# Second expert's rows turned by DMA instead of on the matmul engine, and the second choice's first counts placed sooner

## The chip, the core and the metric

The kernel runs on one core of a Trainium2 chip. A core has a matmul engine (PE, with weight loads PEld beside it), a vector engine (DVE), an activation engine (ACT), GpSimd (POOL), a queue engine (SP) and 16 DMA engines, each with its own stream of instructions that runs in order; they wait for one another through semaphores. The metric is the device time of one execution in microseconds (us), as the median of several runs.

## What is computed

Attention over 8 batches, 12 heads, 448 positions and a head size of 64, then a layer of 8 experts over the 3584 resulting rows of 768 numbers. Each row goes to one expert, and each expert takes 448 rows; the order in which pairs of row and expert are granted is that of their gate logits, over all rows and experts at once.

```python
scores = cap * np.tanh(scale * np.matmul(q, k.transpose(0, 1, 3, 2)) / cap)
attn = np.exp(scores - np.max(scores, axis=-1, keepdims=True))
x = (attn / attn.sum(-1, keepdims=True)) @ v          # 3584 x 768 after reordering
logits = x @ w_gate                                    # 3584 x 8
for idx in np.argsort(-logits.flatten()):
    tok, e = idx // E, idx % E
    if assigned[tok] >= 0 or counts[e] >= N // E: continue
    assigned[tok] = e; counts[e] += 1
for e in range(E):
    mask = assigned == e
    out[mask] = np.maximum(x[mask] @ w1[e], 0) @ w2[e]  # w1: 768 x 1024, w2: 1024 x 768
```

## The kernel before

The first 330 us or so are attention, after which x lies in a DRAM tensor `xs` and the gate logits in SBUF. What follows is a loop over eight choices p = 0 to 7. A choice finds the expert that fills up next and its 448 rows; the expert's two layers are then computed. While PE does the matmuls of choice p, the other engines search for choice p+1 and fetch its weights and rows.

**The search** (class `Routing`) finds thresholds by counting: `select` runs three searches A, B and C. In each round, DVE (line 571) and ACT (line 565) compare all values with a few thresholds and count, one small matmul (line 577) sums the counts over partitions, and DVE (lines 581, 585) derives the next thresholds. Choices 0 and 1 use rounds with 3 thresholds, later ones with 7; `na` of the thresholds go to DVE, the rest to ACT. `finalise` then builds the list of rows: lines 692 and 716 on PE, last line 724, after which DVE writes `idx`.

**The rows of a choice** are gathered from `xs` by four indirect DMAs of POOL (`gather`, line 881) and must then be turned so that the 768 numbers lie on partitions. Two ways stand in the code. `xtr` (line 911) uses PE: four transposes into PSUM for each of six chunks, from which `cutx` (lines 939, 940) makes two float32r halves, `xgh` on ACT and `xgl` on DVE. The other way is used for choices from `FT` on (2 here): `planes` (line 919) lets ACT copy each of the four row tiles apart into 16-bit planes, sends them to DRAM tensors `xz`, and two transposing DMAs on SP (line 922) bring them back into `xg`; `cutt` (line 928 on ACT, then POOL for the first 256 rows and DVE for the rest) converts each of the two halves in two parts. The first matmul of an expert needs the first and the third of these four conversions.

**Each expert** has a first layer, `ffn1`: eight blocks of 18 matmuls of 448 columns (line 978; three products of high and low halves), and a second, `ffn2t`: six blocks of 24 (line 1040): 288 matmuls in all. The weight halves are split by `split1` and `split2` (ACT line 849, then POOL line 856).

**The order of all this is written by hand**, at build time. `tick` is called after each matmul and counts `now`, 320 counts to an expert (144 in the first layer, 176 in the second). The search is a Python generator; each `yield n` says after how many counts its next piece is to be put among the matmuls. `xq`, `bg`, `turnq` and `plan` hold the other pieces with their due counts. Since each engine runs its stream in order, a piece that stands too early in PE's stream makes PE wait. The search of choice 1 runs under expert 0, starting in `tx` and `first`, which turn the first expert's rows and begin its first block.

## Time and profile before

| what | us |
|---|---|
| median of 3 runs (835.54 to 835.95) | 835.9 |
| the profiled execution | 836.45 |
| its span, first to last instruction | 834.7 |
| PE busy in the span | 818.0 |
| DVE busy | 591.9 |
| ACT busy | 566.2 |
| POOL busy | 396.3 |

The profile tells when each instruction started and how long it was busy, and in brackets how long its engine had been idle before and which instruction ended that. The granted clock of PE stands beside each stretch. Matmuls overlap: one of 448 columns is busy for about 0.36 us, but its neighbours start 0.20 us after each other. So where PE is the limit, the distance between starts is what a matmul costs.

### The profile page before, as it was taken

What the parts mean: (1) busy time and instruction counts of PE and PEld (TensorE: products, weight loads), DVE (VectorE), ACT (ScalarE), POOL (GpSimd) and SP (SyncE); (2) the same over time, 40 slices, a digit from 0 to 9 for tenths busy, and PEclk for the clock granted to TensorE, in tenths of its full rate; (3) what the DMA queues carried; (4) which work ended last, traced back from release to release, by engine and by line L of the source; (5) the groups of instructions that cost most, each with busy time, mean ns of one, the idle gap of its engine ahead of it and who ended that gap; (6) DMA issues with size and microseconds to landing.
All of it is one profiled execution on the core that took longest, in us unless ns stands there. A gap on an engine that the chain in (4) does not pass through costs nothing.

```text
span 834.7 us, 16330 instructions
## 1 busy us (share of the span) xinstructions
PE 818.0 (98%) x5790; PEld 570.1 (68%) x5790; DVE 591.9 (71%) x1923; ACT 566.2 (68%) x749; POOL 396.3 (47%) x592
## 2 busy tenths in 40 slices
PE   7999999999999998999999999999999999999997
PEld 3333333333333336788888888888888899999997
DVE  2677899989989868868878779868868874353210
ACT  7999999999999954580783574754755845444510
POOL 8600000000000043591494696676686777787843
PEclk9999999999999999999999999999999999999999
DMA  6433354644635115815546978967968958959814
GB/s 245 159 107 133 111 155 130 203 120 147 200 111 155 41 28 151 293 60 186 167 149 237 256 208 259 321 225 201 300 203 246 294 179 255 317 194 253 254 67 132
DMA packets 116003, 155.55 MB, mean 186 GB/s; under 512 B 66834, under 2 KB 80370, under 8 KB 115922
## 3 DMA queue, kind: packets, MB, share of 16 engines
q1 hardware_dynamic: 108352, 125.19, 49.5%
q0 software_dynamic: 4832, 22.03, 7.9%
q10 hardware_dynamic: 2738, 7.31, 2.3%
q8 instruction: 45, 0.74, 0.4%
q14 instruction: 36, 0.29, 0.1%
HBM read 105.64 MB, written 40.60 MB: 175 GB/s over the span
## 4 chain that ended last, share of the span: by engine, by line
PE 90%; POOL 4%; DVE 3%; DMA 2%; issue 1%; ACT 1%; SPq 0%; DVEq 0%; POOLq 0%; ACTq 0%
PE psH L978 28%; PE psH L1040 24%; PE psX L201 13%; PE psS L161 13%; PE psM L235 3%; PE psS L156 1%; DMA xg<-xz 1%; PE psX L810 1%; POOL out_dram L998 1%; PE psM L257 1%; DVE cmpD L571 1%; PE psX L213 1%; POOL gw L95 1%; DVE cmpD L569 1%; DMA on<-yb 0%
## 5 line engine op out<-in xcount | busy, mean ns | idle before, releaser
L1040 PE MATMUL psH<-hh,w2h 128*128 128x448 f32 x720 | 199.1, 367 | 0.0
L162 ACT ACTIVATE e<-psS 128x896 f32<-128x896 f32 x168 | 146.0, 916 | 13.4 <-PE psS L161 8.7
L167 ACT ACTIVATE e<-e,bias 128x1792 f32<-128x1792 f32 (+2 forms) x74 | 147.2, 1990 | 0.8
L978 PE MATMUL psH<-xgh,w1h 128*128 128x448 f32 (+1 forms) x384 | 141.8, 369 | 0.9 <-ACT xgh L928 0.8
L1040 PEld LDWEIGHTS psH<-hh,w2h 128*128 128x128 f32 x720 | 134.1, 188 | 8.8 <-DVE hh L988 0.5
L978 PE MATMUL psH<-xgh,w1l 128*128 128x448 f32 (+1 forms) x384 | 139.9, 364 | 0.0
L856 POOL TENSOR_TENSOR w1l<-w1r,w1h 128x768 fp32r<-128x768 f32 x62 | 115.3, 1861 | 50.0 <-ACT w1h L849 45.0
L978 PE MATMUL psH<-xgl,w1h 128*128 128x448 f32 (+1 forms) x384 | 135.6, 366 | 0.0
L856 POOL TENSOR_TENSOR w2l<-w2r,w2h 128x768 fp32r<-128x768 f32 x64 | 132.6, 2073 | 6.0 <-ACT w2h L849 4.6
L161 PE MATMUL psS<-tq,tk 64*64 64x448 f32 x1200 | 130.4, 543 | 4.1 <-ACT e L162 4.1
L247 POOL COPY sm<-lgt 32x84 f32<-32x84 f32 x28 | 7.0, 249 | 251.3 <-DVE lgt L245 250.4
L1040 PE MATMUL psH<-hh,w2l 128*128 128x448 f32 x360 | 124.3, 367 | 0.0
L201 PE MATMUL psX<-e,nv 64*64 64x448 f32 x1176 | 121.8, 536 | 0.0
L161 PEld LDWEIGHTS psS<-tq,tk 64*64 64x64 f32 x1200 | 41.4, 132 | 74.6 <-issue 44.3
L201 PEld LDWEIGHTS psX<-e,nv 64*64 64x64 f32 x1176 | 45.7, 133 | 64.8 <-issue 62.5
L978 PEld LDWEIGHTS psH<-xgh,w1h 128*128 128x128 f32 x384 | 72.4, 189 | 6.6 <-ACT xgh L928 1.9
L849 ACT ACTIVATE w2h<-w2r 128x768 fp32r<-128x768 f32 x64 | 76.6, 1210 | 0.3
L978 PEld LDWEIGHTS psH<-xgh,w1l 128*128 128x128 f32 x384 | 72.3, 188 | 4.5
L978 PEld LDWEIGHTS psH<-xgl,w1h 128*128 128x128 f32 x384 | 72.2, 188 | 4.4 <-DVE xgl L940 0.2
L1040 PEld LDWEIGHTS psH<-hh,w2l 128*128 128x128 f32 x360 | 67.6, 188 | 4.2
L987 ACT ACTIVATE hh<-psH 128x448 fp32r<-128x448 f32 x56 | 30.2, 539 | 58.4 <-PE psH L978 55.6
L1044 DVE STREAM_TRANSPOSE yq<-psH 128x448 f32<-128x448 f32 x45 | 35.5, 789 | 37.1 <-PE psH L1040 36.6
(407 smaller groups left out, 1295.3 us busy)
## 6 DMA issues: line engine op xcount, KB each, us to landing
w1r<-in_moe_w_dram SPq DMA_DIRECT2D x64, 384.0 KB, 4.7
w2r<-in_moe_w_dram SPq DMA_DIRECT2D x64, 384.0 KB, 5.5
nv<-in_v_dram SPq DMA_DIRECT2D x24, 448.0 KB, 5.6
tk<-in_k_dram SPq DMA_DIRECT2D x23, 448.0 KB, 3.4
tq<-in_q_dram SPq DMA_DIRECT2D x23, 448.0 KB, 4.3
yb<-yq SPq DMA_DIRECT2D x60, 168.0 KB, 4.5
xs<-Y SPq DMA_DIRECT2D x28, 336.0 KB, 4.5
on<-yb SPq DMA_DIRECT2D x7, 1152.0 KB, 7.5
```

The source lines that it names most:

```text
L95: nc.gpsimd.tensor_copy(gw[hp,p,c:c+8],wgs[hp,p,:])
L161: nc.tensor.matmul(ps[w:w+64,h,:S],tks[g,0][hp,o,r*64:r*64+64],tks[g,1][hp,o,:],start=True,stop=True)
L162: nc.scalar.activation(ev(g,r),ps[:,:,:S],AF.Tanh,scale=sr[0])
L167: act=lambda: nc.scalar.activation(e,e,AF.Exp,scale=sr[1],bias=bias)
L201: for h in range(2): nc.tensor.matmul(avp[g,o][h*64:h*64+64,:S],z[w,r,h,:],ev(g,r)[w,h,:],start=r==0,stop=r==6)
L235: nc.tensor.matmul(ps[k*32:k*32+32,c],lhs,rhs[:,c],start=x<4 and i==0 and b<B-1,stop=b<B-1 and c.stop==S and x==max(y for y in range(end) ...
L849: nc.scalar.activation(view(h),r,AF.Copy)
L856: (eng or nc.gpsimd).tensor_tensor(view(l),r,view(h).bitcast(F32),op=ALU.subtract)
L978: nc.tensor.matmul(ps[:,o:C],a[:,c,:],b[:,c,o:],start=(m==0 and o==0),stop=(m==DC*3-1)); m+=1
L987: nc.scalar.activation(h,ps[:,:C],AF.Relu)
L1040: nc.tensor.matmul(ps[:,:C],spl[p,2,hf,f//2][w][:,f%2,cc*128:cc*128+128],h[a][:,f],start=(m==0),stop=(m==nm-1))
L1044: turnq.append((now[0]+5,now[0]+(5 if p==E-1 else TL),lambda: nc.vector.transpose(yq[p][:,:,hf,cc::3],ps[:,:C])))
```

## The change

`FT` becomes 1: choice 1 also takes the DMA way, and the six calls of `xtr(1, ...)` go. Several places that named choices relative to `FT` now name them directly, so that later ones keep theirs; what follows `FT` still is that choice 1 loads three first-layer weights as soon as its expert is known (`early`), that its first block takes the products without `xgl` first, that choice 2 loads two and not three so early, and that choice 2 now does all counts of its first three A rounds on DVE with longer gaps, as later choices did.

The search of choice 1 does all three counts of each first round (A, B, C) on DVE, places the summing matmul sooner, and loses one count of distance in later rounds. Its keys (`propose_b`) are made, and its first counts started, while the first expert's rows are still being turned; the split of the first expert's second weight tile moves from DVE to POOL.

```diff
-LK=(0,0,112,112,112,112,112,112); FT=2
+LK=(0,0,112,112,112,112,112,112); FT=1
...
-            m=R[i]-1; alone=s.cur>FT and ab=="A" and i<3; na=m if alone else 5 if m==7 else s.na
+            m=R[i]-1; alone=s.cur>FT and ab=="A" and i<3; na=m if alone or s.cur==1 and not i else 5 if m==7 else s.na
...
-            s.pos='A'; yield max(6,12-s.since()) if s.cur==1 and s.since()<20 else 16 if m==7 and s.place()>304 else (24 if s.place()<8 else 18) if m==7 and s.cur==FT+1 and s.place()<32 else 16 if m==7 and s.cur==FT and s.place()<32 else max(13,18-s.since()) if m==7 and s.since()<20 else s.hA+1*(s.cur==1)+(3 if m==7 else 0)+((9 if s.cur>FT+2 and i==1 else 5) if alone and i else 0); s.pos=''
+            s.pos='A'; yield 5 if s.cur==1 and not i else max(6,12-s.since()) if s.cur==1 and s.since()<20 else 16 if m==7 and s.place()>304 else (24 if s.place()<8 else 18) if m==7 and s.cur in (2,3) and s.place()<32 else max(13,18-s.since()) if m==7 and s.since()<20 else s.hA+(3 if m==7 else 0)+((9 if s.cur>4 and i==1 else 5) if alone and i else 0); s.pos=''
...
-                split1(p,1,nc.vector)
+                split1(p,1)
+                rt.propose_b(0,rt.NC)
                 first(n)
         for c in range(n): cutx(p,c,ps[c],256,C)
+        step()
...
                 xtr(0,c+4)
-                if c==1: rt.propose_b(0,rt.NC)
...
-            if p==1 and f==0: work[1]=[lambda: xtr(1,4)]; work[4]=[lambda: xtr(1,5)]
...
-            plan+=[(126,lambda: split1(1,0)),(144,lambda: split1(1,1))]
-            plan+=[(x,lambda c=c: xtr(1,c)) for x,c in ((156,0),(164,1),(172,2),(175,3))]
+            pass
```

On PE, at the end of expert 0's second layer (line 1040, now 1041) and the start of expert 1's first (line 978, now 980), the order before was this; `xg_3569` and `xg_3570` are the two gathered halves of expert 1's rows:

```order
L911 MATMUL psX<-ident,xg_3569 128x128 x2
L911 MATMUL psX<-ident,xg_3570 128x128 x2
L1040 MATMUL psH<-hh,w2l 128x448
L577 LDWEIGHTS r_bo
L577 MATMUL psR<-r_cd_358,r_bo 128x4
L978 MATMUL psH<-xgh,w1h 128x448
L911 MATMUL psX<-ident,xg_3569 128x128 x2
L911 MATMUL psX<-ident,xg_3570 128x128 x2
L978 MATMUL psH<-xgl,w1h 128x448
L978 MATMUL psH<-xgh,w1l 128x448
```

and now, at the same place on PE:

```order
L1041 MATMUL psH<-hh,w2l 128x448
L1041 MATMUL psH<-hh,w2h 128x448 x2
L1041 MATMUL psH<-hh,w2l 128x448
L980 MATMUL psH<-xgh,w1h 128x448
L980 MATMUL psH<-xgh,w1l 128x448
```

The transposes are gone, and the first block begins with the products that need only `xgh`.

On ACT, from the last count of choice 1's search to the end of expert 0's second layer, the order before was this (line 565 are counts, 849 weight splits, 939 conversions of turned rows):

```order
L565 ACTIVATE cmpA,r_cd_357<-r_qt,r_HC 128x252
L565 ACTIVATE cmpA,r_cd_358<-r_VAt,r_T8A 128x252
L849 ACTIVATE w1h<-w1r 128x768
L565 ACTIVATE cmpA,r_ce_350<-r_VAt,r_H8A 128x252 x2
L849 ACTIVATE w1h<-w1r 128x768
L565 ACTIVATE cmpA,r_ce_351<-r_VAt,r_H8A 128x252 x2
L939 ACTIVATE xgh<-psX 128x448 x2
L565 ACTIVATE cmpA,r_cd_358<-r_VAt,r_H8A 128x252
L939 ACTIVATE xgh<-psX 128x448 x3
```

and now, on ACT from the same count on:

```order
L565 ACTIVATE cmpA,r_cd_357<-r_qt,r_HC 128x252
L921 ACTIVATE xgh<-xg_3569 128x1536
L922 DMA xz_61<-xgh 128x1536
L921 ACTIVATE xgl<-xg_3569 128x1536
L922 DMA xz_61<-xgl 128x1536
L921 ACTIVATE xgh<-xg_3570 128x1536
L922 DMA xz_62<-xgh 128x1536
L921 ACTIVATE xgl<-xg_3570 64x1536
L849 ACTIVATE w1h<-w1r 128x768 x2
L565 ACTIVATE cmpA,r_cd_358<-r_VAt,r_H8A 128x252
L930 ACTIVATE xgh<-xg_3569 128x3x256 x2
L930 ACTIVATE xgh<-xg_3570 128x3x192 x2
```

The plane copies (line 919, now 921) and the four conversions (928, now 930) have come in, the conversions in a row; the counts of choice 2's first A rounds have gone from ACT.

On DVE, at the start of expert 0, the order before was this (line 940 subtracts for `xgl`, lines 519 to 531 are `propose_b`, 571 counts):

```order
L856 TENSOR_TENSOR w1l<-w1r,w1h 128x768
L940 TENSOR_TENSOR xgl<-psX,xgh 128x192 x2
L940 TENSOR_TENSOR xgl<-psH,xgh 128x192 x2
L940 TENSOR_TENSOR xgl<-psX,xgh 128x448 x2
L519 TENSOR_SCALAR r_Bt<-r_b 112x32
L520 TENSOR_SCALAR r_Ct<-r_c 112x32
L521 TENSOR_TENSOR r_VB<-r_P,r_Bt 112x256
L522 TENSOR_TENSOR r_VC<-r_P,r_Ct 112x256
L523 TENSOR_TENSOR r_K_372<-r_At,r_Bt 112x32
L531 SCALAR_TENSOR_TENSOR r_K_373<-r_kk,r_Ct 112x32
L571 TENSOR_SCALAR cmpD,r_cd_357<-r_VAt,r_T0A 128x224 x2
```

and now, on DVE at the same place:

```order
L519 TENSOR_SCALAR r_Bt<-r_b 112x32
L520 TENSOR_SCALAR r_Ct<-r_c 112x32
L521 TENSOR_TENSOR r_VB<-r_P,r_Bt 112x256
L522 TENSOR_TENSOR r_VC<-r_P,r_Ct 112x256
L523 TENSOR_TENSOR r_K_372<-r_At,r_Bt 112x32
L531 SCALAR_TENSOR_TENSOR r_K_373<-r_kk,r_Ct 112x32
L942 TENSOR_TENSOR xgl<-psX,xgh 128x192 x2
L942 TENSOR_TENSOR xgl<-psH,xgh 128x192 x2
L571 TENSOR_SCALAR cmpD,r_cd_357<-r_VAt,r_T0A 128x224 x3
L942 TENSOR_TENSOR xgl<-psX,xgh 128x448 x2
```

The counts stand ahead of the last two subtractions, and there are three of them instead of two.

## Rows read from the trace of the kernel before

**Rows 1.** The page's first part: busy time, share, instructions of each engine.

```profile
PE 818.0 (98%) x5790; PEld 570.1 (68%) x5790; DVE 591.9 (71%) x1923; ACT 566.2 (68%) x749; POOL 396.3 (47%) x592
```

**Rows 2.** Timeline of PE, end of expert 0: start us, us busy, instruction, count.

```profile
402.32 0.60 PE L911 MATMUL psX<-ident,xg 128*128 128x128 f32 x4
402.68 0.45 PE L1040 MATMUL psH<-hh,w2l 128*128 128x448 f32 x1
402.96 0.57 PE L1040 MATMUL psH<-hh,w2h 128*128 128x448 f32 x2
```

**Rows 3.** Timeline of PE, expert 1's first matmul and its eighth.

```profile
407.49 0.45 PE L978 MATMUL psH<-xgh,w1h 128*128 128x448 f32 x1
...
409.81 0.37 PE L978 MATMUL psH<-xgh,w1h 128*128 128x448 f32 x1
```

**Rows 4.** Timeline of POOL, first gather of expert 1's rows; in brackets idle before.

```profile
389.24 0.98 POOL L881 DMA_INDIRECT xg<-xs,idx  x1 [13.73 <-DVE zz L734]
```

**Rows 5.** Timeline of POOL, ACT and PE: expert 2's rows (choice 2).

```profile
446.70 0.98 POOL L881 DMA_INDIRECT xg<-xs,idx  x1 [3.70 <-DVE zz L734]
...
466.53 0.84 ACT L928 ACTIVATE xgh<-xg 128x768 fp32r<-128x768 f32 x1 [2.12 <-DMA xg<-xz]
...
468.40 1.98 ACT L928 ACTIVATE xgh<-xg 128x768 fp32r<-128x768 f32 x3
...
468.89 0.37 PE L1040 MATMUL psH<-hh,w2l 128*128 128x448 f32 x1
469.85 0.47 PE L978 MATMUL psH<-xgh,w1h 128*128 128x448 f32 x1 [0.60 <-ACT xgh L928]
```

**Rows 6.** Timeline of POOL, SP and ACT: the rows of choice 6, the seventh.

```profile
684.50 0.99 POOL L881 DMA_INDIRECT xg<-xs,idx  x1 [2.81 <-DVE zz L734]
...
696.76 6.33 SPq L922 DMA_TRANSPOSE xg<-xz  x2
...
702.93 1.58 ACT L928 ACTIVATE xgh<-xg 128x768 fp32r<-128x768 f32 x2 [5.40 <-DMA xg<-xz]
705.17 1.26 ACT L928 ACTIVATE xgh<-xg 128x576 fp32r<-128x576 f32 x2 [0.66 <-DMA xg<-xz]
```

**Rows 7.** Timeline of POOL and ACT: the rows of choice 7, the eighth.

```profile
742.53 0.98 POOL L881 DMA_INDIRECT xg<-xs,idx  x1 [2.27 <-DVE idx L728]
...
764.41 1.26 ACT L928 ACTIVATE xgh<-xg 128x576 fp32r<-128x576 f32 x2 [0.76 <-DMA xg<-xz]
```

**Rows 8.** Timeline of POOL, ACT, PE: choice 3 (the fourth); then the fifth's first matmul.

```profile
506.05 0.98 POOL L881 DMA_INDIRECT xg<-xs,idx  x1 [2.48 <-DVE zz L734]
...
523.91 0.85 ACT L928 ACTIVATE xgh<-xg 128x768 fp32r<-128x768 f32 x1 [0.17 <-DMA xg<-xz]
...
530.68 0.47 PE L978 MATMUL psH<-xgh,w1h 128*128 128x448 f32 x1
...
592.33 0.47 PE L978 MATMUL psH<-xgh,w1h 128*128 128x448 f32 x1 [0.22 <-ACT xgh L928]
```

**Rows 9.** Timeline of DVE and PE, start of expert 0: subtractions, a count, summing matmul.

```profile
345.53 1.38 DVE L940 TENSOR_TENSOR xgl<-psX,xgh 128x448 fp32r<-128x448 f32 x2 [0.72 <-ACT xgh L939]
...
347.91 0.44 DVE L571 TENSOR_SCALAR_CACHE_REDUCE cmpD<-r_VAt,r_T0A 128x224 bf16<-128x224 f16 x1
...
348.27 0.37 PE L978 MATMUL psH<-xgh,w1l 128*128 128x448 f32 x1
348.78 0.18 PE L577 MATMUL psR<-r_cd,r_bo 128*128 128x4 bf16 x1
```

**Rows 10.** Attention matmuls early and late; windows: length, busy by engine, then PEclk.

```profile
4.81 2.47 PE L156 MATMUL psS<-tq,tk 64*64 64x448 f32 x16
...
284.48 1.68 PE L156 MATMUL psS<-tq,tk 64*64 64x448 f32 x16
...
829.30:832.30 3.00, 0.00 (x0) 0.00 (x0) 0.00 (x0) 0.49 (x1) 2.03 (x3) 1.00 0.39 146
832.40:834.70 2.30, 0.00 (x0) 0.00 (x0) 0.00 (x0) 0.00 (x0) 0.00 (x0) 0.50 0.15 53
```

More of the change, by code (lines that the diff above doesn't have):

```diff
@@ L948, in tick @@
         if bc[0]>=BG:
-            if pend and not (cur[0]==FT-1 and 166<now[0]%320<316): bc[0]=0; scatter(*pend.pop(0))
+            if pend and not (cur[0]==1 and 166<now[0]%320<316): bc[0]=0; scatter(*pend.pop(0))
         if len(res)>cur[0]+1 and cur[0]+1 not in xgs:
@@ L955, in tick @@
                 o=(n-1)*320; g=now[0]-o; a=max(262,g+92); b=max(284,g+118)
-                bg.extend((o+x,o+min(y,316),z) for x,y,z in ((a,a+18,lambda: cutt(n,0,0,3)),(a,a+34,lambda: cutt(n,0,3,6)),(b,b+(0 if n==FT else 26),lambda: cutt(n,1,0,3)),(b,b+(7 if n==FT else 22),lambda: cutt(n,1,3,6))))
+                bg.extend((o+x,o+min(y,316),z) for x,y,z in ((a,a+18,lambda: cutt(n,0,0,3)),(a,a+34,lambda: cutt(n,0,3,6)),(b,b+(0 if n<3 else 26),lambda: cutt(n,1,0,3)),(b,b+(7 if n<3 else 22),lambda: cutt(n,1,3,6))))
         while xq and xq[0][0]<=now[0]: xq.pop(0)[1]()
```

## The prediction

> **What bounds the kernel now.** I read the page's busy shares first: the matmul engine (PE) is busy for 98% of the span [rows 1], so time can come from work taken off PE, or from the few waits it still has. Next I read PE's timeline where one expert hands over to the next. At the handover to the second expert there is no wait worth the name: the matmuls of expert 1's last blocks run on, with groups of four transposes (line 911) between them [rows 2, 3]. At the handover to the third, where the rows already come turned by DMA, PE sits idle for 0.60 us until ScalarE (ACT) has converted them [rows 5]. That is the path the second expert is about to get: index found, gather on GpSimd (POOL), four plane copies on ACT, DMA out, transposing DMA back, conversion on ACT, first matmul. The question of this case is how long that path is, against the PE work left when it starts.
>
> **What the change takes off PE.** Six calls of four transposes go, 24 in all. One call stands on PE from 402.32 to the next matmul's start at 402.68, which is 0.36, and the matmul behind it hands on after 0.28 (402.68 to 402.96) where the usual step is 0.20 [rows 2]. So a call costs 0.44 us. Four of the six lie before the second expert's first matmul (407.49): 1.76 us. The other two lie behind it: from 407.49 to 409.81 seven matmuls start, which take 1.40 us by themselves, so the two calls and a short wait cost 0.92 [rows 3]. Together 2.7 us leave PE. The ACT and DVE work of the six conversions was beside PE work and is worth nothing here.
>
> **When the new path starts.** In the order of PE's instructions the last routing matmul of the second choice (L724) stands after 206 matmuls of the first expert before, and after 197 now: nine matmuls of 0.20, or 1.8 us. The gather then starts at 389.24 - 1.8 = 387.4 [rows 4]. I take the whole 1.8: the routing steps stand nine matmuls apart or more in the first layer now as before, and seven or eight apart at the start of the second in both, so each count has the time that it had.
>
> **How long the new path is.** No row shows it for the second choice; the same path of later choices does. From the first gather to the first matmul that it allows: third choice 446.70 to 469.85, 23.15 us, with two counts of the next search standing on ACT between the first conversion and the other three, where the rows leave 1.0 us (466.53 + 0.84 to 468.40) [rows 5]. Seventh choice: 684.50 to the end of the third of four conversions, 705.17 + 1.26/2 = 705.8, which is 21.3 [rows 6]. Eighth: 742.53 to 764.41 + 0.63, which is 22.5 [rows 7]. Fourth: its first conversion started 17.9 us after its gather (506.05 to 523.91) [rows 8]; with the 2.9 us that the seventh needs from first to third conversion (702.93 to 705.8), 20.7. The second choice is most like the seventh and the eighth: in the new order its four conversions stand in a row on ACT, with no count between. I take their middle, 21.9, and keep 20.7 and 23.15 as ends.
>
> **The wait that results.** PE would reach the second expert's first layer at 407.49 - 1.76 = 405.7, 18.3 us after the gather. The path ends at 387.4 + 21.9 = 409.3. So PE waits for 3.6 us (2.4 to 4.9). Before, with its two late calls counted in, that layer stood as if begun at 407.49 + 0.92 = 408.4. **The handover costs +0.9 us** (-0.3 to +2.2): the 2.7 us that were saved are waited away, and some more. Behind the waiting instruction stand the second expert's matmuls and the routing steps between them; ACT waits on the same DMA with nothing else that PE needs, SP holds its next weight loads behind the transposing DMAs as it does for every later choice, and the expert's first two weight splits stand ahead of the conversions on ACT and POOL.
>
> **Later handovers.** The third choice's L724 moves from 177 matmuls to 180 (0.6 us later), the fourth's from 167 to 177 (2.0), the fifth's from 152 to 162, the sixth's from 146 to 150; the rest stay. Third: from the gather to the point where PE would have gone on (468.89 + 0.20 = 469.09) there were 22.4 us, now 21.8, against a path of 20.7 + 1.0 (the two counts between) to 23.15: a wait of 0 to 1.35, in the middle 0.7, where it was 0.76 [rows 5]. That is -0.1 (-0.8 to +0.6). Fourth: its first matmul came at 530.68 with no idle shown, 22.6 us after a gather at 506.05 + 2.0 [rows 8]; its conversions now stand on ACT as the third's did, so the same path gives 0 to 0.5; I take +0.2. The fifth's handover had 0.22 idle on ACT [rows 8], which may go or double; fifth and sixth start their gathers after 162 and 150 matmuls, with 25 us and more left: 0 +/- 0.2.
>
> **The start of the first expert.** The second choice's first count moves ahead of matmul work, and a routing matmul that came 0.51 after its neighbour, not 0.20 (348.27 to 348.78), should come freely: -0.3 at best. Against it three counts of 0.44 at most now stand on DVE ahead of two subtractions that PE needs; DVE had 0.72 idle there, so these come at most 0.6 late [rows 9]. The second weight split goes from DVE to POOL, ahead of the third that POOL did before, and isn't needed until the second block. I take -0.1 (-0.3 to +0.6).
>
> **Sum:** +0.9 - 0.1 + 0.2 + 0 - 0.1 = +0.9 us. The profiled execution took 836.45 us (span 834.7 and 1.75 around it), so 837.35 by it; it lay 0.55 above the median of the three runs, 835.9. The forecast for the median is 836.8.
>
> **Rivals.** *The clock falls in the wait (slower).* This trace shows PE's granted clock at 1.00 until 832.30 and at 0.50, the lower level of 1.2 GHz, from 832.40 on, after PE had been without a matmul since 829.30 [rows 10]. The wait forecast here, 2.4 to 4.9 us, is longer than any that the rows above show inside the expert part. If the clock falls in that wait, the expert's first matmuls take 0.40 instead of 0.20. For how long is bounded by nothing at one end, and at the other by the start of the kernel: sixteen attention matmuls took 2.47 us at 4.81 where they take 1.68 later [rows 10] and that stands in the kernel's first 7.3 us; as much time at the lower level again would cost up to 3.6 us. I take 2.4, the cost of the first two thirds of that: 839.2 us. It decides from a wait near the long end. The Trainium skill states the same direction (TensorE: Matmul & The Clock Gate, Part 1, "The HAM clock gate"): the throttled clock is the default and only activity holds it off. By that rule alone the wait would cost the clock as well; the rows leave it open for a wait of this length, so it is a rival and not the forecast.
>
> *The path is as long as the third choice's* at every handover (23.15): +2.2, +0.6 and +0.5, less 0.1 at the start: +3.2, 839.1. It speaks for it that three weight loads go out shortly before the gather, as there; against it, that no writes of finished rows run beside it.
>
> *The rows come in time (faster)*: then the transposes' 2.7 us is all gain, 833.2. It needs a path of 18.3, which none of the four rows comes near. The Trainium skill (DMA: Bandwidth & Descriptors, "Latency and other measured facts") gives a transposing DMA 261 GB/s; the two here carry 786 KB and 590 KB, so I estimate 5.3 us by that page, and the sum would be about 3 us lower. The trace doesn't agree: from their start at 696.76 to the third conversion at 705.17 it took 8.4 us [rows 6].
>
> *The change doesn't do what it says*: the earlier counts aren't ready when PE reaches them and PE waits there, so the gather starts no sooner; +1.8, 838.6. Against it: the spacing is one that held before.
>
> **How the numbers follow.** Forecast 0.58; clock 0.20; long path 0.10; rows in time 0.07; no sooner start 0.05. A measurement of this kernel tells about 0.2%, 1.7 us, from no change. The forecast's own bounds reach from about 835.3 to 838.2; nearly all of it lies within 0.2%. Faster 0.08 (the rows in time, and a bit), same 0.56, slower 0.36 (clock, long path, half of the rest). The range leaves out the rows in time at the lower end, and at the upper a fallen clock on top of a long path: 835.3 to 839.6.
>
> **What would show it.** In the new profile: no line 911 transposes at 402 to 410; the second choice's gather near 387.4; the first conversion 17.5 to 20 us behind it; an idle row of 2.4 to 4.9 us before the second expert's first matmul, put down to ACT; steps of 0.20 right behind it if the clock held, 0.40 if not; the third expert's wait at 0 to 1.4 us. I am wrong if that idle is under 2 us, or if PE waits before line 577 in the first expert.

## The result and the profile after

The changed kernel takes 841.4 us (median of 5 runs, 839.8 to 842.5) against 835.9 (835.5 to 836.6) before: ratio 1.006, 95% interval 1.0049 to 1.0072. It is slower by 5.5 us, where 0.9 was forecast, and lies beyond the range. The profiled execution took 841.39 us, its span is 839.6; before 836.45 and 834.7, so the traces differ by 4.95. Of all executions behind this document one, of 2098.5 us in the run that takes the causes away with the early DMA, lies far from the others and is left out of its median.

The start of the first matmul of each layer, read from both timelines of PE, gives the length of every layer, with the wait that ends it:

| stage, us | before | after | difference |
|---|---|---|---|
| up to the first expert's first layer | 343.67 | 344.01 | +0.34 |
| first expert, first layer | 30.95 | 31.90 | +0.95 |
| first expert, second layer | 32.87 | 34.47 | +1.60 |
| second expert, first layer | 31.02 | 31.74 | +0.72 |
| second expert, second layer | 31.34 | 31.04 | -0.30 |
| third expert, both | 60.83 | 60.59 | -0.24 |
| fourth expert, first layer | 30.31 | 33.09 | +2.78 |
| fourth expert, second layer | 31.34 | 30.31 | -1.03 |
| all behind | 242.34 | 242.47 | +0.13 |

The first row is no effect of the change that PE shows: up to there it waits nowhere anew, and the kept traces of all versions spread from 342.50 to 344.21 at this point. PE's row of the page says that PE does less and the span is longer, so what came is waiting (before it was [rows 1]):

```profile
PE 817.2 (97%) x5766; PEld 568.7 (68%) x5766; DVE 594.8 (71%) x1934; ACT 567.4 (68%) x735; POOL 402.4 (48%) x598
```

**The second expert's handover** is where I looked first, in PE's timeline (start, us busy, instruction; in brackets the idle time before and its releaser):

```profile
406.62 0.37 PE L1041 MATMUL psH<-hh,w2l 128*128 128x448 f32 x1
410.38 0.74 PE L980 MATMUL psH<-xgh,w1h 128*128 128x448 f32 x1 [3.38 <-ACT xgh L930]
410.92 0.57 PE L980 MATMUL psH<-xgh,w1l 128*128 128x448 f32 x1
411.29 0.57 PE L980 MATMUL psH<-xgh,w1h 128*128 128x448 f32 x1
...
413.16 0.41 PE L980 MATMUL psH<-xgh,w1l 128*128 128x448 f32 x1
413.41 0.18 PE L577 MATMUL psR<-r_cd,r_bo 128*128 128x4 bf16 x1
413.45 0.45 PE L980 MATMUL psH<-xgh,w1h 128*128 128x448 f32 x1
```

PE waits 3.38 us for the conversion. Behind the wait the steps are 0.37 (410.92 to 411.29), not the usual 0.20. The windows of this stretch (length, busy of PE, PEld, DVE, ACT, POOL, then granted clock) say why: the clock went to its lower level, 1.2 GHz, within the wait, and came back at 413.3.

```profile
407.00:409.80 2.80, 0.00 (x0) 0.00 (x0) 0.00 (x0) 1.74 (x3) 1.35 (x1) 1.00 1.14 231
409.90:413.20 3.30, 2.82 (x8) 2.48 (x8) 2.84 (x2) 2.90 (x4) 3.30 (x5) 0.50 0.95 331
413.30:416.00 2.70, 2.65 (x14) 2.09 (x13) 2.65 (x5) 0.00 (x0) 2.70 (x3) 1.00 1.01 396
```

**DVE stands still while POOL subtracts.** At the start of the first expert, DVE, POOL and PE:

```profile
342.72 0.43 DVE L521 TENSOR_TENSOR r_VB<-r_P,r_Bt 112x256 f16<-112x256 f16 x1
343.06 2.03 DVE L522 TENSOR_TENSOR r_VC<-r_P,r_Ct 112x256 f16<-112x256 f16 x1
...
342.79 2.03 POOL L856 TENSOR_TENSOR w1l<-w1r,w1h 128x768 fp32r<-128x768 f32 x1 [0.24 <-ACT w1h L849]
...
345.63 0.36 PE L980 MATMUL psH<-xgl,w1h 128*128 128x192 f32 x1 [0.93 <-DVE xgl L942]
```

Line 522 does the same work as line 521 in the row above and takes 2.03 us instead of 0.43. It ends 0.27 after POOL's subtraction. The subtraction for which PE waits 0.93 us stands behind it. At the second expert the two DVE subtractions of line 932 (0.75 each where nothing is beside them) take 4.65 us, all of it beside POOL:

```profile
410.36 4.65 DVE L932 TENSOR_TENSOR xgl<-xg,xgh 128x576 fp32r<-128x576 f32 x2 [4.63 <-ACT xgh L930]
...
410.25 1.83 POOL L937 TENSOR_TENSOR xgl<-xg,xgh 128x768 fp32r<-128x768 f32 x1
412.02 0.09 POOL L854 MEMSET gap<- 1x1 f32 x1
412.07 2.32 POOL L856 TENSOR_TENSOR w1l<-w1r,w1h 128x768 fp32r<-128x768 f32 x1
```

At the fourth expert the same pair takes 4.20 us, and PE waits 0.94 us for it, then 0.88 and 0.41 for counts queued behind it on DVE. Before, the pair took 1.43 there (first line below), because the rows came earlier and POOL was done.

```profile
530.71 1.43 DVE L930 TENSOR_TENSOR xgl<-xg,xgh 128x576 fp32r<-128x576 f32 x2 [0.18 <-issue]
...
533.65 4.20 DVE L932 TENSOR_TENSOR xgl<-xg,xgh 128x576 fp32r<-128x576 f32 x2 [0.65 <-issue]
...
533.07 1.85 POOL L937 TENSOR_TENSOR xgl<-xg,xgh 128x768 fp32r<-128x768 f32 x1 [0.64 <-ACT xgh L930]
534.86 0.09 POOL L854 MEMSET gap<- 1x1 f32 x1
534.95 2.29 POOL L856 TENSOR_TENSOR w1l<-w1r,w1h 128x768 fp32r<-128x768 f32 x1
...
538.00 0.85 PE L980 MATMUL psH<-xgl,w1h 128*128 128x448 f32 x3 [0.94 <-DVE xgl L932]
```

Not every DVE instruction is held. The counts of line 571, with one input, keep their 0.44 us beside POOL:

```profile
525.82 0.44 DVE L571 TENSOR_SCALAR_CACHE_REDUCE cmpD<-r_VAt,r_H8A 128x224 bf16<-128x224 f16 x1
...
525.40 1.85 POOL L856 TENSOR_TENSOR w1l<-w1r,w1h 128x768 fp32r<-128x768 f32 x1
```

The Trainium skill has this rule (SBUF — State Buffer, "Who interferes with whom"): DVE and POOL share a pair of ports, a DVE instruction with two SBUF inputs contends with a POOL instruction that reads SBUF, and "the other fully blocks" for the whole instruction. The rows above agree: line 522 took 2.03 us instead of 0.43, and line 571, with one input, kept its 0.44. I had not weighed it.

### The profile page after: what moved, and what is told of

Read it like the earlier page. It is cut to its first block, busy times and chain, and to the rows that moved or that the text cites. A ratio compares the mean times of both kernels' runs of the same rounds, so it can differ in the third digit from the quotient of the medians.

```text
span 839.6 us, 16298 instructions
## 1 busy us (share of the span) xinstructions
PE 817.2 (97%) x5766; PEld 568.7 (68%) x5766; DVE 594.8 (71%) x1934; ACT 567.4 (68%) x735; POOL 402.4 (48%) x598
## 4 chain that ended last, share of the span: by engine, by line
PE 89%; POOL 4%; DVE 3%; DMA 1%; issue 1%; ACT 1%; SPq 0%; POOLq 0%; ACTq 0%; DVEq 0%
PE psH L980 28%; PE psH L1041 25%; PE psX L201 13%; PE psS L161 13%; PE psM L235 3%; PE psS L156 1%; PE psX L810 1%; POOL out_dram L999 1%; PE psM L257 1%; DMA xg<-xz 1%; PE psX L213 1%; POOL gw L95 1%; DVE cmpD L569 0%; DMA on<-yb 0%; PE psR L577 0%
## 5 line engine op out<-in xcount | busy, mean ns | idle before, releaser
L856 POOL TENSOR_TENSOR w1l<-w1r,w1h 128x768 fp32r<-128x768 f32 x63 | 117.9, 1872 | 40.8 <-ACT w1h L849 35.2
L988 ACT ACTIVATE hh<-psH 128x448 fp32r<-128x448 f32 x56 | 30.1, 537 | 52.7 <-PE psH L980 49.5
```

What stands on the lines that cost most here:

```text
L856: (eng or nc.gpsimd).tensor_tensor(view(l),r,view(h).bitcast(F32),op=ALU.subtract)
L988: nc.scalar.activation(h,ps[:,:C],AF.Relu)
```

## Experiments

Theory 1: the loss has four parts: the wait, the low clock in it, DVE held by POOL at three places, and the fourth expert's later rows. Rivals: the clock alone, the search order, or a lateness that has nothing to do with POOL. Each median is of 4 to 11 runs; the kernel before lay at 835.5 to 836.5 beside them, and the ratio is to it, with its 95% interval. Each trace is of one execution.

### The start: split back on DVE; small operations later

```diff
-                split1(p,1)
+                split1(p,1,nc.vector)
```

> The changed kernel with one thing undone: the second split of the first expert's weights is on VectorE again, as before, and GpSimd has nothing in that stretch. Theory 1 (VectorE's write of VC, 2.03 us where it took 0.42 before, was held for as long as GpSimd's subtraction of 2.03 us ran beside it): VC takes 0.4 to 0.5 us again; VectorE does the split itself (0.95), so the two subtractions of 128x192 end 0.5 to 0.7 us sooner, TensorE's wait of 0.93 shrinks to 0.2 to 0.5, and the time falls by 0.4 to 0.8 us, to about 840.8. Rival (the sooner order of the choice's work on VectorE is the cost, GpSimd is not): VC stays at 2 us or the wait stays at 0.9 or grows by the 0.95 that VectorE now does more, and the time is 841.4 to 842.4.

Median 839.6 (ratio 1.0051, 1.0037 to 1.0064). Line 522 is back at 0.42 and the wait at 0.40:

```profile
343.54 0.42 DVE L522 TENSOR_TENSOR r_VC<-r_P,r_Ct 112x256 f16<-112x256 f16 x1
...
344.48 0.36 PE L980 MATMUL psH<-xgl,w1h 128*128 128x192 f32 x1 [0.40 <-DVE xgl L942]
```

The first layer took 31.39 us, 0.5 less, as expected. It isn't the 30.95 of before: the wait of 0.40 is left, and it stands in every run that has the small operations ahead of the subtractions and the split on DVE. The median fell by 1.8; of that, 0.9 is in the first expert's second layer (33.59, rows sooner in that execution) and 0.6 lies ahead of the first expert, so neither is an effect of the split that is shown.

```diff
-                rt.propose_b(0,rt.NC)
                 first(n)
         for c in range(n): cutx(p,c,ps[c],256,C)
+        rt.propose_b(0,rt.NC)
         step()
```

> The changed kernel with the six small operations of the second choice (Bt to K) on VectorE behind the subtractions of 128x192 and no longer ahead of them; GpSimd's split stays. Theory 1: VC may still be held by GpSimd's subtraction, but nothing that TensorE waits for stands behind it; the wait of 0.93 at the first expert's fifth matmul goes and the time falls by 0.6 to 1.0 us, to about 840.5. Rival (something else holds the subtraction, its planes or TensorE's transposes): the wait stays above 0.7 and the time is the changed kernel's within 0.3 us.

Median 842.4 (1.0089, 1.0075 to 1.0103): worse, so my expectation failed. Line 522, now later, met POOL's next split and was held again. The first count stood behind it, PE waited 1.71 us for that, and the clock fell (DVE, POOL, PE, then a window):

```profile
344.72 2.06 DVE L522 TENSOR_TENSOR r_VC<-r_P,r_Ct 112x256 f16<-112x256 f16 x1
...
344.55 1.95 POOL L856 TENSOR_TENSOR w1l<-w1r,w1h 128x768 fp32r<-128x768 f32 x1 [0.78 <-ACT w1h L849]
...
348.14 0.16 PE L577 MATMUL psR<-r_cd,r_bo 128*128 128x4 bf16 x1 [1.71 <-DVE cmpD L571]
349.20:352.50 3.30, 3.30 (x9) 2.95 (x10) 1.61 (x9) 2.52 (x5) 0.68 (x1) 0.50 1.01 397
```

The hold stands, the cure was none: what counts is which instruction is behind the held one.

### POOL's splits held away; matmuls in the wait; both

```diff
-                xq.extend(((n-1)*320+248+8*f,lambda f=f: split1(n,f)) for f in range(2))
+                xq.extend(((n-1)*320+248+8*f,lambda f=f: split1(n,f)) for f in range(3 if n==1 else 2))
...
+            if (p,f)==(3,1): work[1]=[lambda: split1(3,2)]
+            if p in (1,3) and f<2: at={**at,0:[],1:[(4,0)]+at[1]}
```

> The changed kernel with GpSimd's splits of weights (w1l of the third chunk, w2l of the first) taken from beside the subtractions on VectorE at the first layers of the second and fourth experts: done sooner for the second, behind the first chunk's ReLU for the fourth. Theory 1 (VectorE's subtraction of 128x576 is held while a subtraction of GpSimd's runs): the second subtraction at each place, 2.38 and 2.40 us, falls to 0.7 to 0.9; the first at each place stays at 1.9 to 2.4, since GpSimd's own part of the rows still runs beside it. At the second expert TensorE gains under 0.2 us, because its low clock (0.50 from 409.83 to 413.25) had it late anyway. At the fourth the wait of 0.94 goes and those of 0.88 and 0.41 shrink: 1.3 to 2.2 us, of which up to 1.0 comes back as waits at the fifth expert, where the changed kernel had regained 1.0. In all 0.5 to 2.0 us less, about 840.2. Rival (the rows of the fourth expert come late, and the exclusion of the two engines costs nothing): the subtractions stay long or TensorE waits as before, and the time stays within 0.3 us of the changed kernel.

Median 838.4 (1.0028, 1.0018 to 1.0039). The pairs of line 932 took 2.99 and 2.55 us (the second is shown), only their first half still held by line 937:

```profile
532.27 2.55 DVE L932 TENSOR_TENSOR xgl<-xg,xgh 128x576 fp32r<-128x576 f32 x2 [0.66 <-issue]
```

The fourth expert's first layer fell from 33.09 to 31.28, the second expert's from 31.74 to 31.44 only, as theory 1 wants. I had expected up to 1.0 to come back at the fifth expert; nothing did (30.31 again). The median fell by 3.0, more than the 0.5 to 2.0 expected; these two layers make 2.1 of it.

```diff
+            if p==1 and f==0: wu[0]=None; warm(7,4)
             ffn1(p,f,work)
```

> The changed kernel with seven matmuls of the identity (128x512, 0.45 us each from start to start) put on TensorE ahead of the second expert's first matmul, to fill most of its wait of 3.4 us; their result is not used. Both theories: the granted clock stays at 1.00 from 406 to 416 and the first matmuls step at 0.20 and not 0.37. Theory 1 (low clock and late xgl cover each other: with full speed TensorE comes to the thirteenth matmul at 412.8 and finds the second subtraction of xgl done only at 415.0): 1.4 to 1.6 us gained at the start come back as a wait of 1.5 to 2.3 us for xgl, and the time falls by 0 to 0.3 us only. Rival (the clock alone made the second expert's first layer longer): the time falls by 1.3 to 1.7 us, to about 839.9.

Median 841.4 (1.0073, 1.0059 to 1.0087). The size was wrong: the seven took 6.17 us, not 3.2, so PE came late by its own work; only the clock can be read (1.00 from 400 to 416). The same with three:

> The changed kernel with three matmuls of the identity ahead of the second expert's first matmul (0.88 us each, as the seven of the run before showed, so 2.6 of the wait's 3.4 us); their result is not used. Both theories: granted clock 1.00 from 406 to 416, first matmuls at 0.20 from start to start. Theory 1 (low clock and held subtraction cover each other): TensorE reaches the sixteenth matmul, the first that needs the second subtraction of 128x576, 1.5 us sooner and waits for it 1.3 to 1.8 us; the time is 841.1 to 841.5. Rival (the clock alone): no such wait, the second expert's first layer falls from 31.7 to 30.4 us and the time to about 840.0.

Median 840.7 (1.0051, 1.0037 to 1.0065). The clock held: eight matmuls and one small one from 409.58 to 411.35 took 1.77 us, where the changed kernel's took 3.07 (410.38 to 413.45). A wait for xgl came in its place:

```profile
409.58 0.48 PE L980 MATMUL psH<-xgh,w1h 128*128 128x448 f32 x1
...
411.35 0.45 PE L980 MATMUL psH<-xgh,w1h 128*128 128x448 f32 x1
...
412.24 0.76 PE L980 MATMUL psH<-xgl,w1h 128*128 128x448 f32 x3
414.36 0.84 PE L980 MATMUL psH<-xgl,w1h 128*128 128x448 f32 x3 [1.37 <-DVE xgl L932]
```

The layer took 31.74 us, what it took with the low clock. (The median is 0.7 lower; 0.8 of this execution's lies in the handover.) With both edits:

> The run with GpSimd's splits held away from the subtractions at the second and fourth experts, and the three matmuls of the identity in the wait as well. Theory 1: now neither cause covers the other; the second expert's first layer falls from 31.4 us (held splits alone) to 30.2 to 30.5, and the time from 838.4 to 837.2 to 837.6. Rival (the clock costs nothing, or the matmuls in the wait themselves delay the layer): 838.2 to 839.0.

Median 836.95 (1.0016, 1.0007 to 1.0025), a little below what was expected. The second expert's first layer in the four cases, one trace each:

| | no matmuls in the wait | three matmuls |
|---|---|---|
| splits as in the changed kernel | 31.74 | 31.74 |
| splits held away | 31.44 | 30.25 |

Taking either cause away alone is worth 0 to 0.3 us, both together 1.5: each hid the other.

### The third choice's pace

Pieces of two long lines:

```diff
-alone=s.cur>FT and
+alone=s.cur>2 and
...
-if m==7 and s.cur in (2,3) and s.place()<32
+if m==7 and s.cur==3 and s.place()<32 else 16 if m==7 and s.cur==2 and s.place()<32
```

> The changed kernel with the third choice's rounds (counts on which engine, distances between rounds) as before; in the changed kernel the constant that turns the second expert's rows to the DMA way also changed them, and the gathers of the experts behind came 4, 12 and 12 matmuls later. Theory 1: the fourth expert's rows come 2.4 us sooner against the fourth expert's start, its subtractions are out of GpSimd's way (none over 2.1 us), and its first layer falls from 33.1 to 30.3 to 31.0 us; 0.5 to 1.0 of that comes back at the fifth expert, as before had it (31.3 us for the fourth's second layer, 30.3 in the changed kernel). In all 1.0 to 2.3 us less: 839.1 to 840.4. Rival (the later gather is not why the fourth expert's first layer is longer): the layer stays at 32.5 or more and the time within 0.4 of 841.4.

Median 840.85 (1.0059, 1.0045 to 1.0072), above the 839.1 to 840.4 expected. The fourth expert's first layer is at 30.31, its second at 31.03, as theory 1 said; but 1.73 and 0.91 us of new waits came in the first expert's second layer. With the old pace two of the third choice's counts are on ACT, where they now stand behind the plane copies of the second expert's rows. So with the sooner search the new pace belongs to the DMA way: it takes those counts off ACT, at the price of the fourth expert's later gather.

### The parts apart

The search alone, on the kernel before (the last line is a piece of a long one):

```diff
+                rt.propose_b(0,rt.NC)
                 first(n)
         for c in range(n): cutx(p,c,ps[c],256,C)
+        step()
...
-                if c==1: rt.propose_b(0,rt.NC)
...
+yield 5 if s.cur==1 and not i else max(6,12-s.since())
```

> The kernel before with the second choice's sooner counts and closer rounds alone; the second expert's rows are still turned by TensorE, the split at the start stays on VectorE, the third choice's rounds stay. Theory 1 (the loss is made of the wait for turned rows, GpSimd beside VectorE at three places and the third choice's pace): none of these is here except a little at the start, where the small operations stand ahead of a subtraction (0.0 to 0.5 us); the time is 835.2 to 836.2, and VC takes 0.4 to 0.5 us. Rival (the sooner order of the second choice disturbs the first expert by itself): 837 or more, with a first expert's first layer of 31.9 us as in the changed kernel, where before had 30.95.

Median 843.3 (1.0093, 1.0078 to 1.0109): I was wrong by 7 us. The profiled execution took 839.7, the fastest of four; the others took 843.2 to 845.0 and have no trace. It waits in four places (1.24, 0.59, 1.19 and 1.18 us), the last behind a DVE instruction held for 2.27. Then the change without the search, against theory 1 too:

> The changed kernel with the second choice's counts and rounds as before (split on VectorE, small operations late), so that the second expert's rows are gathered 11 matmuls, 2.2 us, later; the DMA way and the third choice's new pace stay. Theory 1: the start is as before (0.9 us less than the changed kernel), the rows come 2.2 us later and TensorE's wait grows from 3.4 to 5.2 to 5.8 us; the granted clock falls in it and the first layer stays at 31.5 to 32.5; the fourth expert's first layer is 33 us as in the changed kernel. 842.0 to 843.5. Rival (the sooner search is what cost the 5 us, as the run of the search alone suggests): 837 to 840.

Median 848.0 (1.012, 1.0091 to 1.0148). Two of the six executions took 842.4 and 842.8, which is what I had expected, the others 847.9 to 850.0; the traced one took 849.2. There the wait for the rows was 4.68 us, but the larger loss came at the third expert: the second of its pair on DVE was held through three subtractions of POOL, and PE waited 4.00 us for it.

```profile
475.64 7.10 DVE L930 TENSOR_TENSOR xgl<-xg,xgh 128x576 fp32r<-128x576 f32 x2 [1.81 <-ACT xgh L928]
```

So I took all three parts apart: DMA way (D), search (S), pace (P). Theory 2, formed here, was that search and pace belong together and only the DMA way costs.

> The changed kernel without its DMA way: the second choice's sooner counts and closer rounds and the third choice's new pace, on the kernel before, with the second expert's rows turned by TensorE and the split at the start on VectorE. The gathers of the experts behind come at the counts of before (505, 813, 1115 matmuls). Theory 2 (search and pace belong together: in the run of the search alone VectorE got the second choice's work and the third's old rounds on top of each other; the 5 us of the changed kernel are the DMA way's): 835.0 to 837.0, no wait of TensorE over 0.9 us behind the first expert. Rival (the search is what costs, whatever the pace): 841 or more.

> The kernel before with the third choice's new pace alone. The third expert's rows are gathered at 523 matmuls instead of 505, those behind 11 to 13 later. Theory 2: the third expert's rows come 3 to 4 us late, TensorE waits 3 to 4.5 us at the third expert's first layer, with its clock falling in it: 839 to 844. Rival (the pace is neutral by itself): 835.5 to 837.

> The DMA way alone on the kernel before: the second expert's rows turned by DMA, all choices counted and paced as before (split on VectorE at the start); gathers at 221, 509, 825 matmuls. Theory 2: start as before; rows 2.2 us later than in the changed kernel, so a wait of 4.5 to 5.5 us at the second expert with the clock falling in it, layer 31.5 to 33 us; the fourth expert's layer 33 us from the held subtraction: 842 to 844.5. Rival (the search costs, not the DMA way): 836 to 839.

| parts | median | PE's waits of 0.5 us and more from the first expert on, in order |
|---|---|---|
| none (before) | 835.9 | 0.60 |
| S | 843.3 | 1.24, 0.59, 1.19, 1.18 |
| P | 850.0 | 3.26, 2.92, 2.42, 0.94 |
| D | 842.2 | 2.16, 0.91, 2.29, 0.94, 0.89 |
| S and P | 841.4 | 2.40, 0.78, 0.51 |
| D and S | 840.9 | 0.93, 1.73, 0.91, 2.30 |
| D and P | 848.0 | 4.68, 1.08, 4.00, 0.93 |
| all (after) | 841.4 | 0.93, 3.38, 0.94, 0.88 |

(The waits are those of one execution; for S it is the fastest.) Theory 2 fell: S and P without the DMA way cost as much as all three. It was wrong in part on D and P too: with D alone PE waited 2.29 us for the rows and not 4.5 to 5.5, because it had already waited for counts on ACT, and P alone came to 850.0 where 839 to 844 was expected. Every part alone is slower, and all three together are no worse than S and P. The longest wait of S and P is this, on DVE, POOL and PE, and the window behind it with the low clock:

```profile
392.23 4.07 DVE L513 TENSOR_SCALAR r_b<-r_u 112x32 int32<-112x32 int32 x1
396.22 0.17 DVE L514 TENSOR_SCALAR r_c<-r_u 112x32 int32<-112x32 int32 x1
...
392.60 1.85 POOL L856 TENSOR_TENSOR w1l<-w1r,w1h 128x768 fp32r<-128x768 f32 x1
394.38 0.09 POOL L854 MEMSET gap<- 1x1 f32 x1
394.43 1.82 POOL L856 TENSOR_TENSOR w1l<-w1r,w1h 128x768 fp32r<-128x768 f32 x1
...
398.25 0.68 PE L1041 MATMUL psH<-hh,w2h 128*128 128x448 f32 x2 [2.40 <-DVE yq L1045]
...
398.90:405.60 6.70, 5.92 (x21) 5.29 (x20) 4.98 (x26) 0.00 (x0) 0.00 (x0) 0.50 0.43 161
```

An operation of 0.17 us was held through two POOL subtractions in a row. P alone has the like (line 510, 4.49 us instead of 0.42, beside the same two splits). D and D with S wait for counts on ACT behind plane copies. D alone has the fourth expert's first layer at 33.09 as well, with the third choice's old pace: its second choice is found later, and the fourth's rows are gathered as late as in the changed kernel. To test the cause in S and P, only the two splits were moved:

```diff
-            plan+=[(126,lambda: split1(1,0)),(144,lambda: split1(1,1))]
+            plan+=[(146,lambda: split1(1,0)),(160,lambda: split1(1,1))]
```

> The run search_pace with one thing moved: GpSimd's two splits of the second expert's weights 20 and 16 planning counts later (about 3.7 us). In search_pace they ran from 392.60 to 396.25, and VectorE's first operation of the next choice beside them (a tensor_scalar of 112x32) took 4.07 us instead of 0.17; TensorE waited 2.40 and 0.78 us, and its granted clock was 0.50 for 6.83 us. Theory 3 (all of the loss of search_pace is GpSimd's splits meeting short operations of VectorE): none of the choice's operations over 1 us there, no such wait, no low clock, 5 to 6 us less: 835.3 to 836.8. Rival (the sooner search makes the choice's work meet TensorE's by itself): 838 or more.

Median 837.4 (1.0017, 1.0008 to 1.0026): 4.0 less, not 5 to 6, between theory 3 and its rival. The first split moved by 0.3 us only (392.60 to 392.93), since in both runs it started right behind POOL's last gather, and line 513 was still held for it, 2.26 us. But only for one split: the wait fell from 2.40 to 0.60, and the clock stayed at 1.00.

### The wait itself; the causes taken away together

```diff
-        if j==3:
-            for k,n in ((0,256),(1,192)): nc.sync.dma_start_transpose(...)
+        for k,n in (((0,256),),((1,192),))[j//2] if cur[0]==0 and j%2 else ((0,256),(1,192)) if j==3 else ():
+            nc.sync.dma_start_transpose(...)
```

> The changed kernel with the transposing DMA of the second expert's first 256 rows sent as soon as their two planes are stored, and no longer behind the store of all four; the other transposing DMA keeps its place. It takes the wait itself away instead of what follows from it. In the changed kernel the two went out at 400.79 and 404.1 with 3.3 us of SyncE's queue each; now the first should go at 397 to 398 and the second at 401 to 402, and the last conversion end near 407.5 instead of 410.9. Theory 1: TensorE's wait of 3.4 us falls under 1.0, the granted clock stays at 1.00, the subtractions of 128x576 lie 3 us sooner against TensorE, and the second expert's first layer falls from 31.7 to 30.3 to 30.9 us: 3.3 to 4.4 us in all up to the second layer, of which nothing comes back later, since the fourth expert's loss (2.8) and the fifth's gain (1.0) stay; the time is 837.0 to 838.2. Rival (the transposing DMAs are slowed by the loads and the row stores beside them, whenever they are sent): the rows land less than 1.5 us sooner and the time is 839.5 or more.

Median 842.8 (1.008, 1.0067 to 1.0093): the edit did not do what I meant. On SP:

```profile
399.89 3.13 SPq L924 DMA_TRANSPOSE xg<-xz  x1
403.14 0.56 SPq L922 DMA_DIRECT2D xz<-xgl  x1
405.99 2.54 SPq L924 DMA_TRANSPOSE xg<-xz  x1
```

The second plane's store was issued at 396.08 and the first transposing DMA still went only at 399.89. The view of DMAs says why: the store took 3.7 us to land (384 KB, in us from issue to landing), so it landed at about 399.8.

```profile
xz<-xgl ACTq DMA_DIRECT2D x1, 384.0 KB, 3.7
```

The transposing DMA then kept the last store behind it until 403.14, and the second transposing DMA waited for that. The rows came 1 us later, PE waited 4.38 us, and the time rose by 1.4.

> The run with the sooner transposing DMA, together with the split back on VectorE at the start and GpSimd's splits held away from the subtractions at the second and fourth experts: each cause that the runs have shown is taken away, the change's own saving of 2.7 us of transposes kept. Theory 1: the parts add up: 0.5 at the start, 3.3 to 4.4 at the second expert, 1.8 at the fourth, from 841.4: 834.7 to 836.0, against 835.9 for the kernel before. Rival (what is taken away at one place comes back at another): 836.5 or more.

Median 840.3 (1.0048): the early transposing DMA again, with a wait of 3.88 us; the sum could not be tested with it. (With the early DMA at all experts: 841.5, where 0.6 less to 0.5 more than this run was expected; a miss.) So with the DMAs as they were:

> The changed kernel with the causes taken away that the runs have shown, and none added: split on VectorE at the start, GpSimd's splits held away from the subtractions at the second and fourth experts, two matmuls of the identity (1.8 us) in the second expert's wait; the transposing DMAs as in the changed kernel. Theory: 0.5 less at the start than the run with held splits and three matmuls (836.95), and the wait at the second expert 0.5 to 0.9 shorter, as the run with the split on VectorE had it: 835.7 to 836.5, which is the kernel before within 0.1%. Rival (the wait for the rows comes back to the changed kernel's length or the two matmuls leave the clock to fall): 837 or more.

Median 837.1 (1.0015, 1.0006 to 1.0024), 0.6 above what I wanted, like the run without the start's edit. In its trace 0.68 us of wait are left at the second expert beside 1.8 of idle matmuls, 0.41 at the start, and 0.46 and 0.18 at the fourth expert.

> The changed kernel with the causes taken away, and with work in the wait in place of idle matmuls: split on VectorE at the start and the small operations of the second choice behind the subtractions there; GpSimd's splits held away at the second and fourth experts; the first twelve products of the second expert's first chunk in two halves by rows, so that the 256 rows that land first (1.3 to 2 us ahead of the others) are multiplied while the others are still converted. Theory: 0.3 to 0.4 less at the start than the run best (837.1), 1.0 to 1.5 less at the second expert, clock at 1.00 throughout: 835.2 to 836.0, at or just under the kernel before. Rival (the rows land so close together that the halves bring under 0.5, or the clock falls in the wait that is left): 836.6 or more.

Median 840.0 (1.0042, 1.0029 to 1.0056): the small operations, put behind the subtractions, met POOL's next split once more (line 522: 2.05 us) and PE waited 1.70 for the count. The halves let PE begin in the wait, but it then waited 0.87 for a subtraction held by line 937, and 1.36 at the third expert. No version beats the kernel before.

## Why the prediction was wrong

**The new path: right.** The second choice's gather was forecast at 387.4 and came at 388.59, which is 387.3 with the 1.29 taken off by which that execution was late when the layer began. From the gather to the first matmul it took 21.8 us; 21.9 was forecast from [rows 6, 7]. The wait was 3.38 against 3.6. That it fits to 0.1 is luck, the band is not: the same way took 20.6 to 21.2 in three versions that left its DMAs and the counts on ACT alone (s_late, s_dve, hold13). One reading was off. The second line of [rows 3] is the seventh matmul, not the eighth, so six steps of 0.20 lie between, and the two late calls cost 1.12, not 0.92. With that the forecast for the handover would have been +0.7; it cost +0.5 (1.60 - 1.12).

**The clock: a rival at 0.20 that came true, at half its price.** "I take 2.4" was too much: up to 413.45 the low clock cost 1.3 us (3.07 against 1.77). That the start of the kernel, from which the price was scaled, ran at the lower level was inferred there from matmul times; no row of the granted clock shows it. Against the layer's 29.9 without its late transposes (31.02 - 1.12) it became 1.8 longer, and 1.5 of this goes when both causes are taken away. But the four cases above show that this is not the clock's own: the held subtraction would have cost as much with the clock at full speed. The Trainium skill's rule, which I had left as a rival, agrees with the row (0.50 behind a wait of 3.38).

**The start of the first expert: the step that failed first.** I wrote that the subtractions behind the counts on DVE "come at most 0.6 late", and that the second weight split "isn't needed until the second block". The split's result indeed was not needed; its running was the harm. I costed the move from DVE to POOL by who waits for it, and not by what it keeps DVE from. The layer measured +0.95, forecast -0.1 (up to +0.6). The hold is 0.51 of it, which goes with the split back on DVE (31.90 to 31.39). The other 0.44 stays there and is gone only with the small operations behind the subtractions and the split on DVE (30.95 with D alone): that part lies within the 0.6.

**The fourth expert: +2.8 where "the same path gives 0 to 0.5".** I looked at the later gather only for its effect on the first matmul. That was right: the handover itself moved by -0.04. But conversions that come later put DVE's part beside POOL's, and this was not in the sum: 1.8 of the 2.8 go with POOL's splits held away, all of it with the sooner gather (30.31 in the run of the pace). It could have been read: before, the pair of line 930 at 469.83 took 2.60 us, its first half beside a POOL subtraction, where it took 1.43 at 530.71 with nothing beside it. There PE didn't need it yet.

```profile
469.83 2.60 DVE L930 TENSOR_TENSOR xgl<-xg,xgh 128x576 fp32r<-128x576 f32 x2 [1.50 <-ACT xgh L928]
...
469.31 1.84 POOL L935 TENSOR_TENSOR xgl<-xg,xgh 128x768 fp32r<-128x768 f32 x1
```

**The third handover** (-0.30, forecast -0.1) was within its bounds. **The fifth** brought -1.03, forecast 0: the idle time before its first matmul, of which the prediction says that it "may go or double", went (0.22 in [rows 8], none below). The fourth expert's second layer takes 30.3 us where the fifth's rows are gathered after 162 of its matmuls (the changed kernel, D alone, P alone) and 31.0 and more where after 152 (before, S and P, the run of the pace); with S alone, after 146, it takes 30.1. So it goes with the place of the gather and not with the pace alone; by what way is not shown.

```profile
597.15 0.39 PE L980 MATMUL psH<-xgh,w1h 128*128 128x448 f32 x1
```

**The sum.** +0.5 +1.8 -0.3 -0.2 +2.8 -1.0 +0.95 +0.3 +0.1 = 4.95. Terms that I had put down at -0.1 and +0.2 make 3.7 of it; low clock and held subtraction at the second expert, which had no term, 1.5 to 1.8.

**Shown and not shown.** That DVE is held by POOL is shown by taking POOL's splits away; it costs 0.5 at the start and 1.8 at the fourth expert. That clock and subtraction hide each other is shown by the four cases. Why the search alone waits at its four places was not taken apart, except for one held instruction. Why the same path takes up to 1 us more or less in different kernels stays open.

## What to carry to other kernels

When an operation moves from DVE to POOL, ask not only who needs its result but which DVE instructions with two SBUF inputs, or short tensor_scalar ones, will run beside it, and what stands behind them: 0.2 us of work was held for up to 4 us. Where a wait on PE and a late operand end at about the same time, take both away in one run before calling either harmless. And when a constant switches one expert to another way, list everything else that reads it: here it changed the pace of the third choice, which neither went without the DMA way nor came free with it.

## What the hardware showed unexpectedly

- A held DVE instruction can stay out between two POOL subtractions that follow each other closely: 4.07 us for line 513 through two (1.85 and 1.82 us), 4.49 for line 510, and the second of a pair through three (the pair 7.10). It isn't always so: at the second expert the first half of line 932 got in when line 937 ended (it was done 0.61 later), and POOL's next subtraction was the one that lost. What decides it is not shown. A plain tensor_scalar of 112x32 int32 was held as well as tensor_tensor.
- POOL loses time too: line 856 beside line 932 took 2.29 to 2.32 us, alone 1.85.
- The length of PE's wait alone doesn't say whether the granted clock falls: it fell behind a wait of 1.71 us at the start of the first expert, and stayed at 1.00 behind one of 1.70 at the same place and for the same count in the last run, and behind one of 1.73 in the first expert's second layer (the run of the pace).
- A transposing DMA went out 3.8 us after its store had been issued (396.08 to 399.89), 3.7 of it until the store had landed, and kept SP's queue for 2.5 to 3.1 us. Its place in that queue matters as much as its length.
